# Attention feeding a capacity-limited expert layer: a coarse-grid routing search with an exact count, and row turning moved to VectorE

## The chip, the cores and the metric

The kernel runs on one core of one Trainium2 chip. A core has a matrix engine (TensorE, "PE" in the profile; its weight loads are "PEld"), three elementwise engines (VectorE "DVE", ScalarE "ACT", GpSimd "POOL"), a queue engine that issues transfers (SyncE, "SP" or "SPq"), an on-chip memory of 128 partitions, a matmul result memory (PSUM) and 16 DMA engines that reach DRAM. Every engine works through its own list of instructions in order; semaphores order them against each other. The metric is device time in microseconds of one execution.

## The reference

```python
def _attn_ref(q, k, v):                     # 8 batches, 12 heads, 448 tokens, 64
    scores = scale * np.matmul(q, k.transpose(0, 1, 3, 2)) - np.log(S)
    attn = 1.0 / (1.0 + np.exp(-scores))
    return np.matmul(attn, v)

def _moe_ref(x, w_gate, w1, w2):            # x: 3584 tokens x 768; 8 experts, 768 -> 1024 -> 768
    cap = N // E                            # 448
    logits = x @ w_gate
    order = np.argsort(-logits.flatten())
    for idx in order:                       # best (token, expert) pair first
        tok, e = idx // E, idx % E
        if assigned[tok] >= 0 or counts[e] >= cap: continue
        assigned[tok] = e; counts[e] += 1
    for e in range(E):
        mask = assigned == e
        out[mask] = np.maximum(x[mask] @ w1[e], 0.0) @ w2[e]
```

The attention uses a sigmoid in place of a softmax. Its output, one row of 768 numbers per token, goes to the expert layer. Each of the 3584 tokens goes to one of 8 experts, and each expert takes exactly 448, in the order of all logits. All values are 32-bit floats.

## The kernel before, in words

**Attention.** 48 pairs of heads (8 batches of 6) run one after the other. For a pair, VectorE turns k and q (`kqT`, L408), ScalarE and VectorE split them into a high and a low part (`kqH` L416, `kqL` L417), TensorE forms the scores (L433, L443), ScalarE the sigmoid (L423), TensorE the product with v (L457, L463), and VectorE copies the result to `xt` (L465, L467). `xt` holds a batch with its 768 features on partitions. A short list `bg` holds work that is slipped in, one item for each pair: the logits of a finished batch (L478, L480), and for batch 0 the function `rows`: three transposes on TensorE (L489), a copy, and after two of them a store of 112 token rows to the DRAM tile `xs` (L496). For the other seven batches (`LATE = 7`) these 56 items wait in the list `late`.

**Routing** goes in eight phases; a phase finds the expert that fills first among those left. `keys` gives a token's logit to its best expert and a very low number to the others, and two transposes put the keys of the experts on partitions (`r_KE`, 16 partitions for each expert). `search` finds, for all experts at once, the bit pattern of the 448th largest key, two bits a step, in 16 steps: three counts of keys at or above a threshold (L178, each followed by a read of its accumulator), a sum over the expert's 16 partitions (in phase 0 a small matmul, L190; later two VectorE transposes and a reduce, L194 to L200), and the next thresholds (L202 to L217). `pick` takes the expert with the highest threshold (L229 to L250), `place` and `lists` (L257 to L298) make the list of its 448 tokens.

**Phase 0 stands alone** between attention and experts. In its loop (L563) some of the `late` items are put on TensorE and ScalarE after every step: one before, seven after the keys, three after each search step. When the expert is known, SP reads its number (`value_load`, L585) and issues the loads of its weights (L592); when the list is known, GpSimd gathers the token rows (L625), and `xturn` transposes them back on TensorE (L639) and splits them (L642 on ScalarE, L643 on VectorE).

**Experts.** Eight times, 144 matmuls for the first layer (L734, L736, L738) and 144 for the second (L771, L773, L775). The order of everything else is fixed when the program is written out, by a clock that adds 189 for each matmul: at `t_route` the next piece of the routing of a later phase is put in, then the clock must advance by the number the piece returned (`T_STEP`, `T_DVE`, `T_PICK` and so on) plus `SLACK`; `chores` hold the gathers and `xturn`s of the next expert and the transposes of finished outputs (L652), with a due time each, one in 1000. `prepare` enters the gathers and turns of the next expert as soon as its list is known; what is left at the end of an expert is put out by `flush`.

Of the kernel before, what the change touches and what calls it, by code (L numbers as in the profile page):

```python
# [7 lines left out]
F32 = mybir.dt.float32  # L8
F32R = mybir.dt.float32r
BF = mybir.dt.bfloat16  # L10
# [12 lines left out]
LATE = 7  # L23
XT_BUFS = 7
# [5 lines left out]
T_KEYS, T_KE, T_STEP, T_DVE, T_KAP, T_PICK, T_TOT, T_OH, T_BT = 3600, 2100, 2050, 2025, 500, 2600, 600, 3800, 600  # L30
# [6 lines left out]
Y_DVE, Y_WAIT = 6, 4000  # L37

# [10 lines left out]
def route_consts(nc, cp, K):  # L49
# [59 lines left out]
    g = 0  # L109
# [6 lines left out]
    K.gfin = _s32(g)  # L116


class Router:
# [4 lines left out]
    def __init__(self, tc, K, st, wk, psum):  # L124
# [5 lines left out]
        tc.nc.vector.memset(self.csum, -28.0)  # L130

# [30 lines left out]
    def search(self, pe):  # L162

        nc, K, wk, KT = self.nc, self.K, self.wk, self.KT
        p = self.bank()
        for g in range(2):
            nc.tensor.transpose(p[:, g * 112:(g + 1) * 112],
                                KT[:, g].rearrange("p e c -> p (e c)"), K.ident[:112, :112])
        KE = wk.tile([128, 224], F32, name="r_KE")
        nc.vector.tensor_copy(KE, p[:, :224])  # L170
        T, JP = K.c0, None
        X = None if pe else self.bank().bitcast(I32)
        for st in range(16):
            sh = 30 - 2 * st
            cnt = wk.tile([128, 3], BF, name="r_cnt") if pe else K.CN
            for i in range(3):
                junk = wk.tile([128, 224], BF, name="r_junk")
                nc.vector.tensor_scalar(junk, KE, T[:, i:i + 1].bitcast(F32), None, OP.is_ge, OP.add,  # L178
                                        accum_out=cnt[:, i:i + 1])
            nX = None  # L180
            if 0 < st < 15:
                nX = wk.tile([128, 3], I32, name="r_X") if pe else X[:, 4 * (st % 2):4 * (st % 2) + 3]
            acc = wk.tile([128, 1], F32, name="r_acc")
            j2 = wk.tile([128, 3], F32, name="r_j2")
            if pe:
                if nX is not None:
                    nc.vector.tensor_scalar(nX, K.kk[:, st + 1], JP, None, OP.bitwise_xor)
# [4 lines left out]
            else:  # L192
                ct = wk.tile([128, 32], F32, name="r_ct")
                nc.vector.transpose(ct, cnt)  # L194
                if nX is not None:
                    nc.vector.tensor_scalar(nX, K.kk[:, st + 1], JP, None, OP.bitwise_xor)
                s2 = wk.tile([128, 2], F32, name="r_s2")
                nc.vector.tensor_reduce(s2, ct.rearrange("p (e r) -> p e r", r=16), AX.X, OP.add)
                ct2 = wk.tile([128, 32], F32, name="r_ct")
# [19 lines left out]
            if not pe:  # L219
                yield T_DVE  # L220
# [666 lines left out]
```

## Time and profile before

| | |
|---|---|
| median of 3 runs | 882.02 us (881.35 to 885.34) |
| the profiled execution | 883.43 us, span 881.7 us, mean granted clock 0.987 |
| attention | from 0 to 278.6 us |
| phase 0 of the routing, first loads, gather and turns | 278.6 to 332.8 us |
| experts | 332.8 to 861 us |
| the last rows out | 861 to 881.7 us |
| busy: PE, DVE, ACT, POOL | 840.1, 542.4, 447.3, 466.0 us |
| bytes read, written in DRAM | 96.76 MB, 24.31 MB |

The stages are read off the instructions in order of time: the last logits of attention stand at 278.7 us, the first expert matmul at 332.8 us. A busy TensorE need not be at its full rate, since its matmuls overlap and their ends are modelled. In the rows "x18" counts instructions that were merged, the bracket behind a row gives the idle time of its engine before it and what ended it, and a row of a stretch gives, for each engine, microseconds busy and the number of instructions, then the granted TensorE clock (1.00 is full), the share of the DMA engines that was busy, and GB/s.

### The profile page before, as it was taken

What the parts mean: (1) busy time and instruction counts of PE and PEld (TensorE: products, weight loads), DVE (VectorE), ACT (ScalarE), POOL (GpSimd) and SP (SyncE); (2) the same over time, 40 slices, a digit from 0 to 9 for tenths busy, and PEclk for the clock granted to TensorE, in tenths of its full rate; (3) what the DMA queues carried; (4) which work ended last, traced back from release to release, by engine and by line L of the source; (5) the groups of instructions that cost most, each with busy time, mean ns of one, the idle gap of its engine ahead of it and who ended that gap; (6) DMA issues with size and microseconds to landing.
All of it is one profiled execution on the core that took longest, in us unless ns stands there. A gap on an engine that the chain in (4) does not pass through costs nothing.

```text
span 881.7 us, 16211 instructions
## 1 busy us (share of the span) xinstructions
PE 840.1 (95%) x5467; PEld 636.9 (72%) x5467; DVE 542.4 (62%) x2060; ACT 447.3 (51%) x612; POOL 466.0 (53%) x446
## 2 busy tenths in 40 slices
PE   6999999999999739998999999999999999999996
PEld 3455555555554528987988988988888888999996
DVE  4566555555554988958859879779779631332130
ACT  6777677777775734434434434534434344541420
POOL 9744344444410014854864873873883883851561
PEclk9999999999999979998999999999999999999999
DMA  9866766666621855443442442551542542634643
GB/s 173 165 142 149 153 126 127 127 126 127 126 43 54 270 192 154 120 138 123 128 136 97 160 155 81 177 162 57 189 153 72 170 153 90 209 96 141 203 151 126
DMA packets 213811, 122.16 MB, mean 139 GB/s; under 512 B 153344, under 2 KB 202496, under 8 KB 213728
## 3 DMA queue, kind: packets, MB, share of 16 engines
q1 hardware_dynamic: 200992, 87.62, 38.2%
q0 software_dynamic: 10880, 33.28, 12.0%
q8 instruction: 43, 0.70, 0.3%
q10 hardware_dynamic: 1856, 0.23, 0.2%
q14 instruction: 40, 0.33, 0.1%
HBM read 96.76 MB, written 24.31 MB: 137 GB/s over the span
## 4 chain that ended last, share of the span: by engine, by line
PE 82%; DVE 11%; issue 2%; DMA 2%; POOL 1%; SPq 1%; ACT 1%; POOLq 0%; DVEq 0%; ACTq 0%
PE tp L457 13%; PE sc L433 11%; PE sc L736 9%; PE sc L734 9%; PE sc L738 9%; PE sc L773 6%; PE sc L775 6%; PE sc L771 6%; DVE r_junk L178 4%; PE tp L463 2%; PE sc L443 2%; PE tp L639 2%; PE tp L652 2%; PE tp L478 1%; PE rt L289 1%
## 5 line engine op out<-in xcount | busy, mean ns | idle before, releaser
L605 POOL TENSOR_TENSOR wl<-wr,wh 128x768 fp32r<-128x768 f32 (+1 forms) x96 | 204.9, 2145 | 124.5 <-ACT wh L603 116.8
L423 ACT ACTIVATE at<-sc,bias 128x896 f32<-128x896 f32 x168 | 161.5, 1006 | 67.1 <-PE sc L443 38.4
L383 POOL DMA_DIRECT2D nkq<-in_q_dram x188 | 118.4, 646 | 116.2 <-DVE kqT L408 104.6
L775 PE MATMUL sc<-hh,wl 128*128 128x448 f32 (+2 forms) x400 | 150.2, 375 | 0.0
L738 PE MATMUL sc<-xh,wl 128*128 128x448 f32 (+2 forms) x396 | 146.2, 369 | 0.0
L736 PE MATMUL sc<-xl,wh 128*128 128x448 f32 (+2 forms) x396 | 146.0, 369 | 0.1
L773 PE MATMUL sc<-hl,wh 128*128 128x448 f32 (+2 forms) x400 | 145.5, 364 | 0.2 <-POOL hl L746 0.2
L734 PE MATMUL sc<-xh,wh 128*128 128x448 f32 (+2 forms) x396 | 145.0, 366 | 0.0
L771 PE MATMUL sc<-hh,wh 128*128 128x448 f32 (+2 forms) x400 | 144.1, 360 | 0.4 <-issue 0.4
L178 DVE TENSOR_SCALAR_CACHE_REDUCE r_junk<-r_KE,r_T 128x224 bf16<-128x224 f32 x315 | 123.2, 441 | 0.1
L603 ACT ACTIVATE wh<-wr 128x768 fp32r<-128x768 f32 (+1 forms) x112 | 102.0, 939 | 36.3 <-DMA wr<-in_moe_w_dram 23.4
L457 PE MATMUL tp<-at,nv 128*64 128x448 f32 x576 | 118.8, 548 | 0.0
L746 POOL TENSOR_TENSOR hl<-yt,hh 128x896 fp32r<-128x896 f32 x32 | 68.4, 2136 | 48.8 <-ACT yt L745 47.2
L742 ACT ACTIVATE hh<-sc 128x896 fp32r<-128x896 f32 x32 | 29.5, 921 | 117.1 <-PE sc L738 117.1
L417 DVE TENSOR_TENSOR kqL<-kqT,kqH 128x896 fp32r<-128x896 f32 (+1 forms) x49 | 52.5, 1073 | 58.5 <-ACT kqH L416 58.4
L773 PEld LDWEIGHTS sc<-hl,wh 128*128 128x128 f32 x400 | 75.8, 189 | 6.8 <-issue 1.1
L625 POOL DMA_INDIRECT xr<-xs,r_idx x32 | 32.0, 999 | 91.2 <-ACT wh L603 80.2
L736 PEld LDWEIGHTS sc<-xl,wh 128*128 128x128 f32 x396 | 75.2, 190 | 6.7 <-issue 0.5
L457 PEld LDWEIGHTS tp<-at,nv 128*64 128x64 f32 x576 | 37.1, 136 | 59.1 <-issue 56.6
L734 PEld LDWEIGHTS sc<-xh,wh 128*128 128x128 f32 x396 | 75.2, 190 | 6.0
L771 PEld LDWEIGHTS sc<-hh,wh 128*128 128x128 f32 x400 | 76.0, 190 | 4.8 <-issue 0.6
L738 PEld LDWEIGHTS sc<-xh,wl 128*128 128x128 f32 x396 | 75.1, 190 | 5.3
(166 smaller groups left out, 1266.1 us busy)
## 6 DMA issues: line engine op xcount, KB each, us to landing
wr<-in_moe_w_dram SPq DMA_DIRECT2D x64, 384.0 KB, 3.0
wr<-in_moe_w_dram SPq DMA_DIRECT2D x48, 512.0 KB, 3.6
nkq<-in_k_dram SPq DMA_DIRECT2D x192, 56.0 KB, 2.6
xs<-xr SPq DMA_DIRECT2D x32, 336.0 KB, 3.3
nkq<-in_q_dram POOLq DMA_DIRECT2D x188, 56.0 KB, 2.7
nv<-in_v_dram SPq DMA_DIRECT2D x92, 96.0 KB, 2.7
ys<-yt SPq DMA_DIRECT2D x20, 112.0 KB, 1.9
nr<-in_v_dram SPq DMA_DIRECT2D x46, 32.0 KB, 2.2
```

Source lines behind the costliest of these rows:

```text
L178: nc.vector.tensor_scalar(junk, KE, T[:, i:i + 1].bitcast(F32), None, OP.is_ge, OP.add, accum_out=cnt[:, i:i + 1])
L383: qn.dma_start(t[o:o + 32, n], rws[x])
L423: nc.scalar.activation(a, p[:, :, :S], AF.Sigmoid, bias=bias, scale=1 / math.sqrt(D))
L457: nc.tensor.matmul(p[j * 64:j * 64 + 64, :S], nat["v", b, g][:, h0 + j, c, :], AT[b, pr, c][:, j, :], start=(c == 0), stop=(c == 2 and pr ...
L603: nc.scalar.activation(hi, raw[u], AF.Copy)
L605: eng.tensor_tensor(lo, raw[u], hi.bitcast(F32), OP.subtract)
L734: nc.tensor.matmul(ph[:, f, lo:hi], wh[:, a, fs], xh[:, dd, lo:hi], start=st, stop=False)
L736: nc.tensor.matmul(ph[:, f, lo:hi], wh[:, a, fs], xl[:, dd, lo:hi], start=False, stop=False)
L738: nc.tensor.matmul(ph[:, f, lo:hi], wl[:, a, fs], xh[:, dd, lo:hi], start=False, stop=en)
L771: nc.tensor.matmul(py[:, d2, :w], wh[:, a, dsl], h1, start=st, stop=False)
L773: nc.tensor.matmul(py[:, d2, :w], wh[:, a, dsl], h2, start=False, stop=False)
L775: nc.tensor.matmul(py[:, d2, :w], wl[:, a, dsl], h1, start=False, stop=(j == 1 and a == 3))
```

## The change

**Search.** Thresholds are now numbers on a grid, not bit patterns. `scale`, which runs once in the attention, takes `D`, the power of two at or below the largest logit of batches 0 to 3. Phase 0 starts at -2D with steps of D and refines four times by 4 (`N_FIRST`), so it ends on a multiple of D/64. Each later phase starts at the last phase's threshold less D and takes nine steps (`N_FAST`), down to D/262144. Each step has three counts, the sum, and three small operations, as before. Then one more count at the point found (`count(base)`) gives the exact number of keys at or above it.

**Pick.** Thresholds and counts are spread over the partitions by a transpose and a matmul; `pick` leaves out experts with fewer than 448, takes the highest, and adds the counts of those that have this threshold. If the sum is exactly 448, the tokens above the threshold are the expert's tokens. VectorE reads this sum into a register (`value_load`) and branches: if it is not 448, `exact` does the former 16-step search in one piece on VectorE.

**Rows.** Batches 0 to 6 are no longer transposed by TensorE. After every second pair `turn_rows` does one VectorE transpose of 32x32 blocks (128x2x448, 896 numbers on each partition), three for a batch; it writes every sixth number of the tile `xz` (24 bytes apart), and after the third SP stores the batch with four transfers. A token's row in `xs` now has its 768 features in another order (feature r*128+c at 6c+r), so that `xturn` reads its operand with a step of six numbers, and the `late` rows of batch 7, the only ones left (`LATE = 1`), are copied into this order too.

**Order.** `T_PICK` is 7000 in place of 2600, `T_KAP` 1500 in place of 500, and `prepare` enters gathers and turns no earlier than 33000 into an expert (`X_AT`), the first expert excepted. Tiles: `xt` 3 buffers in place of 7, `xz` 2.

```diff
-LATE = 7
-XT_BUFS = 7
+LATE = 1
+XT_BUFS = 3
+XZ_BUFS = 2
-T_KEYS, ..., T_KAP, T_PICK, ... = 3600, 2100, 2050, 2025, 500, 2600, 600, 3800, 600
+T_KEYS, ..., T_KAP, T_PICK, ... = 3600, 2100, 2050, 2025, 1500, 7000, 600, 3800, 600
+N_FIRST, N_FAST = 4, 9
+FOUND = 0x43E00000
+X_AT = 33000
...
-        for st in range(16):
+    def search(self, k):
+        pe = k == 0
+        rows = range(N_FIRST) if pe else range(1, N_FAST + 1)
...
+        for r in rows:
+            cnt = wk.tile([128, 3], BF, name="r_cnt") if pe else K.CN
+            for i in range(3):
+                self.count(T[:, i:i + 1], cnt[:, i:i + 1])
...
+            nc.vector.tensor_scalar(j2, tot, 447.5, None, OP.is_ge, OP.add, accum_out=acc)
+            if more:
+                T = wk.tile([128, 3], F32, name="r_T")
+                nc.vector.scalar_tensor_tensor(T, acc.to_broadcast([128, 3]), K.kw[:, r, :1], nX, OP.mult, OP.add)
+            nb = wk.tile([128, 1], F32, name="r_base")
+            nc.vector.tensor_scalar(nb, acc, K.kw[:, r, :1], base, OP.mult, OP.add)
+            base = nb
+            if more and not pe:
+                yield T_DVE
+        self.base = base
+        self.cnt = wk.tile([128, 1], BF, name="r_cn1")
+        self.count(base, self.cnt)
...
     def pick(self):
-        nc.tensor.transpose(p[:112, :128], self.kap.to_broadcast([128, 112]), K.ident)
+        nc.tensor.transpose(p[:, :128], self.base.to_broadcast([128, 128]), K.ident)
+        nc.tensor.matmul(p[:, 128:256], self.cnt.to_broadcast([128, 128]), K.G, start=True, stop=True)
+        nc.vector.tensor_scalar(few, cr, 447.5, NONE, OP.is_lt, OP.mult)
+        nc.vector.tensor_tensor(kr, tr, few, OP.subtract)
         nc.vector.tensor_reduce(km, kr, AX.X, OP.max)
+        nc.vector.tensor_tensor(few, cr, few, OP.add)
+        nc.vector.scalar_tensor_tensor(few, kr, km, few, OP.is_equal, OP.mult)
+        nc.vector.tensor_reduce(ok, few, AX.X, OP.add)
+        found = nc.vector.value_load(ok[:1].bitcast(I32))
+        with self.tc.If(found != FOUND):
+            self.exact(kr)
+            nc.vector.tensor_reduce(km, kr, AX.X, OP.max)
...
+        def turn_rows(b, pr):
+            if pr == 1:
+                XR[b] = xa.tile([128, S // 32, 32, NP], F32, name="xz", bufs=XZ_BUFS)
+            nc.vector.transpose(XR[b].rearrange("p i j r -> p r i j")[:, pr - 1:pr + 1],
+                                XT[b][:, pr - 1:pr + 1].rearrange("p r (i t) -> p r i t", t=32))
+            if pr == NP - 1:
+                for a in range(4):
+                    nc.sync.dma_start(xs[b * S:(b + 1) * S, 192 * a:192 * a + 192].rearrange("(i t) c -> t i c", t=32),
+                                      XR[b][32 * a:32 * a + 32].rearrange("t i j r -> t i (j r)"))
...
+            if old and old[1] % 2 and old[0] < B - LATE:
+                bg.append(lambda b=old[0], pr=old[1]: turn_rows(b, pr))
...
-                nc.tensor.transpose(p[:, i * n:(i + 1) * n], xg[kx, j][:n, dd * 128:(dd + 1) * 128], ident[:n, :n])
+                nc.tensor.transpose(p[:, i * n:(i + 1) * n], xg[kx, j][:n, dd::NP], ident[:n, :n])
...
             def prepare():
-                t0 = clock[0]
+                t0 = max(clock[0], start + X_AT) if kx else clock[0]
```

**VectorE at the end of phase 0**, before: the last of 16 search steps and the pick (`r_junk` is a count, `r_km` the highest threshold).

```order
L178 TENSOR_SCALAR r_junk,r_cnt<-r_KE,r_T 128x224 x3
L202 TENSOR_SCALAR r_j_3968,r_acc<-rt 128x3
L217 TENSOR_SCALAR r_J<-r_acc,r_J 128x1
L222 TENSOR_SCALAR r_kap<-r_J 128x1
L232 TENSOR_REDUCE r_km<-rt 112x1
L234 SCALAR_TENSOR_TENSOR r_w_3998<-rt,r_km,c_rank 112x8
```

And now: the last of 4 steps and the pick, to the branch over `exact`.

```order
L183 TENSOR_SCALAR r_junk,r_cnt<-r_KE,r_T 128x224 x3
L233 TENSOR_SCALAR r_j_3514,r_acc<-rt 128x3
L238 TENSOR_SCALAR r_base<-r_acc,c_kw,c_base_2069 128x1
L183 TENSOR_SCALAR r_junk,r_cn_3520<-r_KE,r_base 128x224
L290 TENSOR_SCALAR r_few<-rt 128x8
L291 TENSOR_TENSOR r_kr<-rt,r_few 128x8
L293 TENSOR_REDUCE r_km<-r_kr 128x1
L294 TENSOR_TENSOR r_few<-rt,r_few 128x8
L295 SCALAR_TENSOR_TENSOR r_few<-r_kr,r_km,r_few 128x8
L297 TENSOR_REDUCE r_ok<-r_few 128x1
L298 TENSOR_LOAD r_ok
L299 COMPARE_AND_BRANCH
```

Twelve steps are gone; one count, five small operations, a register load and a branch stand before the row that was L234 and is L304 now.

**TensorE at the end of expert 0**, before: the last second-layer matmuls of expert 0, the turns of expert 1's rows (`xr`), and the first-layer matmuls of expert 1.

```order
L639 MATMUL tp<-ident,xr 128x128 x3
L775 MATMUL sc<-hh,wl 128x448
L771 MATMUL sc<-hh,wh 128x448
L773 MATMUL sc<-hl,wh 128x448
L775 MATMUL sc<-hh,wl 128x448
L639 MATMUL tp<-ident,xr 128x128 x9
L639 MATMUL tp<-ident,xr 128x64 x6
L734 MATMUL sc<-xh,wh 128x448
```

And now, where the last two of the eight turns stand.

```order
L872 MATMUL sc<-hl,wh 128x448
L738 MATMUL tp<-ident,xr 128x64 x3
L874 MATMUL sc<-hh,wl 128x448
L870 MATMUL sc<-hh,wh 128x448
L872 MATMUL sc<-hl,wh 128x448
L874 MATMUL sc<-hh,wl 128x448
L870 MATMUL sc<-hh,wh 128x448
L872 MATMUL sc<-hl,wh 128x448
L738 MATMUL tp<-ident,xr 128x64 x3
L874 MATMUL sc<-hh,wl 128x448
```

Five of the eight turns stood behind the last matmul of expert 0; now all eight stand among its matmuls, six apart, the last well before its end.

**VectorE in the attention**, now: the work of two pairs, with the turn of `xt` between the copy of one pair and the turn of k and q for another.

```order
L536 COPY xt<-tp 128x448
L589 STREAM_TRANSPOSE xz<-xt 128x2x448
L479 STREAM_TRANSPOSE kqT<-nkq 128x896
L488 TENSOR_TENSOR kqL<-kqT,kqH 128x896
L536 COPY xt<-tp 128x448
L538 TENSOR_TENSOR xt<-tp,xt 128x448
```

Before, the same rows stood there without `xz`, and in batch 1's time a copy of `rows` after some of them. The logits of a finished batch, which were the first item slipped in behind it, are now the second, one pair later.

More of the change, by code (lines that the diff above doesn't have):

```diff
@@ L116, in route_consts @@
     K.gfin = _s32(g)
+    K.cw = cp.tile([128, N_FAST + 1, 3], F32, name="c_cw")
+    for r in range(N_FAST + 1):
+        nc.vector.tensor_scalar(K.cw[:, r], t8, 4.0 ** -r, None, OP.mult)
 class Router:
@@ L160, in keys, with ends @@
         self.KT = KT
-    def search(self, pe):
-        nc, K, wk, KT = self.nc, self.K, self.wk, self.KT
+    def ends(self):
+        nc, KT = self.nc, self.KT
         p = self.bank()
@@ L167, in search @@
             nc.tensor.transpose(p[:, g * 112:(g + 1) * 112],
[L168 to L172, printed above, removed]
-        for st in range(16):
-            sh = 30 - 2 * st
+                                KT[:, g].rearrange("p e c -> p (e c)"), self.K.ident[:112, :112])
+        self.KE = self.wk.tile([128, 224], F32, name="r_KE")
@@ new lines, in ends, with count, sums @@
+        nc.vector.tensor_copy(self.KE, p[:, :224])
+    def count(self, T, cnt):
+        junk = self.wk.tile([128, 224], BF, name="r_junk")
+        self.nc.vector.tensor_scalar(junk, self.KE, T, None, OP.is_ge, OP.add, accum_out=cnt)
+    def sums(self, cnt, ct, s2, ct2, between=None):
+        nc = self.nc
+        nc.vector.transpose(ct, cnt)
+        if between:
+            between()
+        nc.vector.tensor_reduce(s2, ct.rearrange("p (e r) -> p e r", r=16), AX.X, OP.add)
+        nc.vector.transpose(ct2.rearrange("p (e r) -> p e r", r=16), s2[:, :, None].to_broadcast([128, 2, 16]))
+        return ct2[:, :3]
@@ L185, in search @@
             if pe:
[L186 to L187 removed]
+                ahead()
                 yield T_STEP
@@ L192, in search @@
             else:
[L193 to L199, printed above, removed]
-                nc.vector.transpose(ct2.rearrange("p (e r) -> p e r", r=16), s2[:, :, None].to_broadcast([128, 2, 16]))
@@ L225, in pick @@
+        nc.vector.tensor_copy(f[0], nX[:, :1].bitcast(F32).to_broadcast([128, 32]))
+        nc.vector.transpose(f[1], f[0])
+        for q in range(4):
+            for o in range(4):
+                nc.vector.tensor_copy(kr[32 * o:32 * o + 32, 2 * q:2 * q + 2], f[1][32 * q:32 * q + 32, ::16])
     def pick(self):
@@ L329, in phase @@
             yield T_KEYS
-            yield from self.search(k == 0)
+            self.ends()
+            yield from self.search(k)
             yield T_KAP
```

106 lines of the change are left out of this document (70 added, 36 removed).

## The prediction

> **What bounds the kernel now.** I read the chain of waits first, then the stretches of the stages, then each stage's instructions in time. The first row below is the chain's share by engine, then come the stretches of the first three stages (PE, PEld, DVE, ACT and POOL busy, clock, DMA share, GB/s), with two short ones that are used later.
>
> ```profile
> PE 82%; DVE 11%; issue 2%; DMA 2%; POOL 1%; SPq 1%; ACT 1%; POOLq 0%; DVEq 0%; ACTq 0%
> ```
>
> ```profile
> 0.00:278.60 278.60, 270.40 (x2216) 137.88 (x2216) 152.91 (x210) 200.34 (x220) 128.30 (x220) 1.00 0.62 125
> 278.60:332.80 54.20, 34.27 (x257) 22.89 (x257) 44.72 (x222) 29.14 (x61) 4.13 (x6) 0.87 0.69 220
> 332.80:861.00 528.20, 522.35 (x2891) 463.76 (x2890) 342.69 (x1625) 215.65 (x325) 329.48 (x213) 0.99 0.44 137
> 320.00:325.00 5.00, 1.32 (x34) 1.05 (x34) 3.23 (x8) 1.63 (x2) 0.00 (x0) 0.50 0.46 157
> 405.00:410.00 5.00, 4.68 (x15) 4.07 (x16) 4.09 (x23) 1.42 (x3) 1.86 (x2) 0.50 0.01 2
> ```
>
> TensorE sets the pace of attention (270.4 of 278.6 us busy, the rest is the start) and of the experts (522.4 of 528.2). Only in the 54 us between them does it wait, and there VectorE is busy 44.7. This stretch is phase 0, one dependent chain. Its rows in time: the first count, the second step, the last step, its end, the threshold, the highest threshold, and the operation behind it.
>
> ```profile
> 285.12 0.45 DVE L178 TENSOR_SCALAR_CACHE_REDUCE r_junk<-r_KE,c_c 128x224 bf16<-128x224 f32 x1
> ...
> 287.66 0.45 DVE L178 TENSOR_SCALAR_CACHE_REDUCE r_junk<-r_KE,r_T 128x224 bf16<-128x224 f32 x1
> ...
> 313.51 0.44 DVE L178 TENSOR_SCALAR_CACHE_REDUCE r_junk<-r_KE,r_T 128x224 bf16<-128x224 f32 x1
> ...
> 315.16 0.21 DVE L217 TENSOR_SCALAR r_J<-r_acc,r_J 128x1 int32<-128x1 int32 x1
> 315.40 0.15 DVE L222 TENSOR_SCALAR r_kap<-r_J 128x1 int32<-128x1 int32 x1
> ...
> 315.97 0.17 DVE L232 TENSOR_REDUCE r_km<-rt 112x1 f32<-112x8 f32 x1 [0.41 <-PE rt L229]
> 316.17 0.23 DVE L234 SCALAR_TENSOR_TENSOR r_w<-rt,r_km,c_rank 112x8 f32<-112x8 f32 x1
> ```
>
> From 287.66 to 313.51 are 14 steps, 1.846 us each, and L234 starts 31.05 us after the first count. What follows is a chain too, by the chain's own rows: nothing of the weights or rows is asked for before the pick, so it moves with it.
>
> ```profile
> 320.44 3.76 DMA wr<-in_moe_w_dram
> ...
> 326.70 4.49 DMA xr<-xs,r_idx
> ```
>
> **The change, part by part.**
>
> *Search and pick of phase 0.* The new steps have the same counts, the same matmul and as many small operations, so three cost 1.846 each, 5.54 (the old first step, 2.54, had three operations that are gone). The fourth runs to its last operation as the old last step did (313.51 to 315.16, plus 0.2: 1.85). Then one count more with its read (0.55); the hop to TensorE and back (from 315.40, where the old threshold was formed, to 315.97: 0.55); six small operations at the 0.20 between 315.97 and 316.17, with some of them longer (1.3); a register load and a branch. SP loads a register from the same kind of tile, in the row of the load and the register operation behind it (shortest/median/longest in ns, then first and last start):
>
> ```profile
> L585 SPq TENSOR_LOAD <-r_ei x8: 266/278/481, 318.4 to 796.1; - x8
> L585 SPq FUSED_REGOPS  x8: 152/157/181, 319.0 to 796.4; - x8
> ```
>
> From 318.4 to 319.0 is 0.6 us, and 0.15 for the compare; with the jumps 0.9. No row shows a jump. Below I bound it by nothing, above by the 1.9 us that the shortest of the profile's transfers takes to land, as if code had to be fetched:
>
> ```profile
> ys<-yt SPq DMA_DIRECT2D x20, 112.0 KB, 1.9
> ```
>
> I take 0.15, the register operation's row, as both are sequencer work. [...]
>
> Sum: 5.54 + 1.85 + 0.55 + 0.55 + 1.3 + 0.9 = 10.7 in place of 31.05, a gain of 20.35. TensorE has no late rows left to do in these steps, so it falls to the clock of the 320 to 325 row (0.50), and its five small matmuls on the chain, 0.16 to 0.32 us each, grow by about 0.3 in all. **Gain 20.0**, with bounds 18 and 20.5.
>
> *Rows of batch 0 off TensorE.* Eight groups of three transposes stood in the attention; the first and the last:
>
> ```profile
> 56.40 0.54 PE L489 MATMUL tp<-ident,xt 128*112 128x128 f32 x3
> ...
> 95.92 0.54 PE L489 MATMUL tp<-ident,xt 128*112 128x128 f32 x3
> ```
>
> 8 × 0.54 = 4.3, on the pace-setter. `scale` gives some back once: TensorE waits for the 0.62 copy (below), two small VectorE operations, and does one transpose, with hops 1.7. **Gain 2.6.** The 48 other groups ran under the search and pay nothing by going.
>
> *Rows by VectorE.* 21 transposes of 896 numbers. Each goes between a copy (L465) and the next kqT; around that place:
>
> ```profile
> 240.65 0.62 DVE L465 COPY xt<-tp 128x448 f32<-128x448 f32 x1 [0.53 <-PE tp L457]
> ...
> 241.19 1.10 DVE L408 STREAM_TRANSPOSE kqT<-nkq 128x896 f32<-128x896 f32 x1
> ...
> 243.37 1.09 DVE L417 TENSOR_TENSOR kqL<-kqT,kqH 128x896 fp32r<-128x896 f32 x1 [1.08 <-ACT kqH L416]
> ...
> 246.62 0.47 PE L433 MATMUL sc<-kqH 64*128 64x448 f32 x2
> 246.84 1.01 ACT L423 ACTIVATE at<-sc,bias 128x896 f32<-128x896 f32 x1 [1.71 <-PE sc L443]
> ```
>
> The same transpose with contiguous writes takes 1.10, and with writes 8 bytes apart, on the outputs of the last experts, 1.12:
>
> ```profile
> L669 DVE STREAM_TRANSPOSE yt<-sc x5: 1117/1119/1119, 792.9 to 861.7; 128x896 f32<-128x896 f32 x5
> ```
>
> The lower bound is 1.10, the upper, for 24 bytes apart, twice that. kqL, 1.10 later, ends at 245.6, and the scores that need it start at 246.62. ScalarE waits 1.1 for kqH and then has 1.71 idle. So kqL comes 1.0 us before TensorE asks for it, and kqT could be 2.1 late in all. I put it at **nothing**, by the L669 row; at 2.2 each it would cost 0.1 × 21 = 2.
>
> *Stores.* SP now has 28 issues in the attention, before 4. Eight loads of k, in as many pieces each as a store has, take it 4.18 us, 0.52 each; and from 40 to 250 us it waits (us in total, times, longest) on kqT alone 26 us:
>
> ```profile
> 74.61 4.18 SPq L383 DMA_DIRECT2D nkq<-in_k_dram  x8
> ```
>
> ```profile
> SPq L383 <- DVE kqT L408: 26.2, 13, 3.2
> ```
>
> 28 × 0.52 = 15 fits into 26. Behind a store on SP's queue stand the loads of k and v for pairs three to four ahead, some 17 us before their use (278.6 / 48 = 5.8 for a pair). **Nothing**, with the DMA engines themselves left to a rival.
>
> *End of expert 0.* Expert 1's list came late, so five of its eight turns stood in a row after expert 0:
>
> ```profile
> 400.44 0.36 PE L775 MATMUL sc<-hh,wl 128*128 128x448 f32 x1
> 401.88 1.01 PE L639 MATMUL tp<-ident,xr 128*128 128x128 f32 x6 [1.08 <-DVE xl L643]
> ...
> 405.83 0.74 PE L734 MATMUL sc<-xh,wh 128*128 128x448 f32 x1
> ```
>
> From 400.64, where the next matmul was due, to 405.83 are 5.2 us; spread out, five turns cost 0.33 each (below), 1.7, so 3.5 are lost. Then the clock is at half: 15 matmul records in the row from 405 to 410, where 5 us hold 24, 2.0 more. With 9 steps in place of 16 the list of expert 1 is out 8,000 to 10,000 of the clock's units sooner, and the order has the turns among the matmuls. **Gain 5.5**, bounds 3 and 6.
>
> *Later phases.* The six later searches lose 42 steps, but VectorE (342.7 of 528.2 busy) is not the bound there: nothing. Their branches hold VectorE 0.9 us each, twice just ahead of turns: **loss 0.5**, bounds 0 and 12 (six times the 2 us).
>
> *Turns with a step of six numbers.* 64 groups of three transposes now load weights 24 bytes apart. What a group costs now is read between matmuls:
>
> ```profile
> 725.36 0.37 PE L773 MATMUL sc<-hl,wh 128*128 128x448 f32 x1
> 725.56 0.49 PE L639 MATMUL tp<-ident,xr 128*128 128x128 f32 x3
> ...
> 726.09 0.36 PE L771 MATMUL sc<-hh,wh 128*128 128x448 f32 x1
> ```
>
> 725.36 to 726.09 less two matmuls at 0.20 is 0.33. The nearest rows with a step are the weight loads of the second layer, contiguous in expert 3 (560 to 592 us, first row) and 8 bytes apart in expert 6 (800 to 812, second); mean ns behind the comma:
>
> ```profile
> L771 PEld LDWEIGHTS sc<-hh,wh 128*128 128x128 f32 x22 | 4.1, 188 | 0.3
> ```
>
> ```profile
> L771 PEld LDWEIGHTS sc<-hh,wh 128*128 128x128 f32 x19 | 3.7, 194 | 0.2
> ```
>
> 3% more. Bounds: nothing, and a doubling, 64 × 0.33 = 21. I take **nothing**, the end that these rows are nearest to. [...]
>
> **Sum.** 883.4 - 20.0 - 2.6 - 5.5 + 0.5 = 855.8 for an execution like the profiled one. That one stood 1.4 above the median, so 854.4; I say **855**. The bounds that do not belong to a rival make it 850 to 862.
>
> **The rivals.**
>
> *The branch is taken.* I worked the reference's logits out in double precision from its inputs. D is 2^-6 (largest logit 0.01696). Phase 0 finds its grid point easily, and five later phases have a gap of 2.7e-7 or more, or none behind the 448th key, against a grid of 6.0e-8. In phase 4 the gap between keys 448 and 449 is 4.0e-8; a grid point lies in it, 1.2e-8 above the lower key. Logits larger by two parts in a million miss it. Then `exact` holds VectorE for 16 steps of the pitch in these chain rows, 2.33 us, and 20 small copies, 41 us:
>
> ```profile
> 657.17 1.11 DVE r_junk L178 x6
> 659.50 1.11 DVE r_junk L178 x6
> ```
>
> The order puts this pick 0.41 of an expert into expert 2, its turns for expert 3 at 0.75; an expert takes 68 us, so the turns wait until 1.01, some 17 us of TensorE, and then come in a burst that costs some 3 as at 400 us. 855 + 20 = **875**. For it: the narrow margin. Against: the sigmoid's error must be one-sided and of that size.
>
> *The step of 24 bytes costs* (the slower rival). Place: the weight loads of the turns, in line with TensorE's matmuls, and VectorE's new transposes. Price, where each takes f times as long: 21 × (f - 1) us for the turns, and 21 times what 1.1 × f exceeds 2.1 by. 1.5 gives 866, 2 gives **878**, and from 2.2 (25 + 6) the kernel is slower than before, 886. For it: no row has a step as long. Against: 188 and 194, 1.10 and 1.12. [...]
>
> *The DMA engines.* The stores of batches 0 to 6 come in 12,544 pieces of 768 bytes. Two rows show what a packet takes, of loads in the attention (100 to 250 us) and of the old stores (282 to 315): packets, MB, share of 16 engines.
>
> ```profile
> q1 hardware_dynamic: 77625, 12.76, 45.7%
> ```
>
> ```profile
> q1 hardware_dynamic: 3294, 8.88, 83.2%
> ```
>
> 14 ns for 164 bytes, 133 for 2,700. By bytes a piece of 768 takes 38 ns, in all 30 us of 16 engines, 0.11 of the stage; at 133 ns it would be 104 us, 0.37, which with the 0.62 there now makes 1.0. Then loads come 1 to 2 us late for each of six batches: **865**. For it: k's loads stand behind the stores on one queue. Against: shorter pieces take less time.
>
> **How the numbers follow.** The forecast 0.61; branch taken 0.18; the step 0.14 (0.03 of it slower, 0.04 no change); DMA engines 0.05; others 0.02. The range reaches from 848, where the rest of the experts' 5.8 us without TensorE goes too (some 3 us), to **877**, to take in the taken branch; the forecast's own is 850 to 862. A difference under 0.5% (877.6 to 886.4 is no change) can't be told from none: faster 0.91, same 0.05, slower 0.04.
>
> **What would show it.** Four steps of 1.85 us between attention and the experts, and 10 to 11 us from the first count to L304; attention 2 to 3 us shorter with TensorE never waiting on kqL; no burst of L738 near 400 us and no clock of 0.5 after it; a group of L738 at 0.49; no `x_f` tile at work anywhere. A run of L183 counts without pauses in expert 2, an L738 group at 0.7 or more, or a `xz` transpose above 2.1 us would make the forecast wrong.

## The result: slower, 896.0 us where 855 was predicted

The changed kernel takes 896.0 us (median of 4 runs, 891.0 to 897.4) beside 882.3 for the kernel before: 1.0144 times as long, interval 1.0102 to 1.0186. The profiled execution took 897.4 us with a span of 895.6, against 881.7. Four rows of TensorE in time cut both spans into the same stages: the last logits of attention and the last block of second-layer matmuls, before and after (the experts' first matmul stands at 332.80 before and at 324.69 now).

```profile
278.71 0.59 PE L478 MATMUL tp<-xt,wgz 128*32 128x112 f32 x16 [0.82 <-DVE xt L467]
872.24 0.36 PE L771 MATMUL sc<-hh,wh 128*128 128x192 f32 x1 [0.41 <-issue]
```

```profile
286.97 0.59 PE L549 MATMUL tp<-xt,wgz 128*32 128x112 f32 x16 [0.82 <-DVE xt L538]
324.69 0.56 PE L833 MATMUL sc<-xh,wh 128*128 128x256 f32 x1
886.14 0.36 PE L870 MATMUL sc<-hh,wh 128*128 128x192 f32 x1 [0.41 <-ACT yt L802]
```

| stage (us) | before | after | difference | predicted | missed |
|---|---|---|---|---|---|
| attention, to the last logits | 278.7 | 287.0 | +8.3 | -2.6 | 10.9 |
| to the experts' first matmul | 54.1 | 37.7 | -16.4 | -20.0 | 3.6 |
| to the last block of the experts | 539.4 | 561.5 | +22.0 | -5.0 | 27.0 |
| rest | 9.5 | 9.5 | 0 | 0 | 0 |

So the search did become shorter, and more than that was lost before and behind it.

**Attention loses its time in the first 40 us**, before `xz` is first stored. Stretches of the kernel before, then of the changed one (columns as in the prediction: PE, PEld, DVE, ACT, POOL busy, clock, DMA share, GB/s):

```profile
0.00:20.00 20.00, 12.51 (x78) 7.35 (x80) 8.29 (x10) 12.68 (x16) 19.16 (x37) 1.00 0.91 170
30.00:40.00 10.00, 10.00 (x74) 4.94 (x72) 5.63 (x10) 7.64 (x9) 6.27 (x11) 1.00 0.91 181
```

```profile
0.00:20.00 20.00, 10.31 (x58) 5.38 (x58) 6.74 (x9) 10.22 (x13) 17.77 (x35) 1.00 1.17 144
30.00:40.00 10.00, 6.51 (x34) 2.90 (x30) 6.50 (x6) 6.02 (x7) 6.17 (x17) 0.83 0.80 137
100.00:250.00 150.00, 148.07 (x1217) 75.16 (x1215) 104.48 (x119) 112.39 (x122) 67.68 (x108) 1.00 0.94 164
```

TensorE has done 20 matmuls fewer by 20 us, and 40 fewer between 30 and 40, where its clock drops. The DMA engines are busier and move less: 144 GB/s at a share of 1.17, against 170 at 0.91. The rows of that start: the changed kernel's two waits for operands of the scores, then the load queue's own row over the first 45 us (packets, MB, share), of the changed kernel and of the one before.

```profile
33.36 0.47 PE L504 MATMUL sc<-kqH 64*128 64x448 f32 x2 [2.84 <-ACT kqH L487]
34.49 0.47 PE L504 MATMUL sc<-kqL,kqH 64*128 64x448 f32 x2 [0.65 <-DVE kqL L488]
```

```profile
q1 hardware_dynamic: 25310, 3.52, 73.7%
```

```profile
q1 hardware_dynamic: 29936, 4.32, 57.0%
```

16 engines for 45 us, times the share, by the packets: 21 ns a packet of 139 bytes now, 13.7 for 144 bytes before. The loads are the same; their destinations are not. The change's new small tiles (constants, and those of `exact`) stand ahead of the tiles of q, k and v and move these by 1,600 bytes: `nkq` began at byte 57,600 of a partition, a multiple of 256, and begins at 59,200, 64 bytes past one.

**The routing before the experts.** VectorE's rows: the first count, the sum of the proof, and the operation behind the branch; then the sequencer's load, compare and the semaphore behind the jump (shortest/median/longest in ns, first and last start).

```profile
294.31 0.45 DVE L183 TENSOR_SCALAR_CACHE_REDUCE r_junk<-r_KE,c_T 128x224 bf16<-128x224 f32 x1
...
303.96 0.16 DVE L297 TENSOR_REDUCE r_ok<-r_few 128x1 f32<-128x8 f32 x1
307.88 0.23 DVE L304 SCALAR_TENSOR_TENSOR r_w<-r_kr,r_km,c_rank 112x8 f32<-112x8 f32 x1 [3.76 <-DVEq L299]
```

```profile
L298 DVEq TENSOR_LOAD <-r_ok x7: 315/320/547, 304.2 to 603.0; - x7
L299 DVEq COMPARE_BRANCH  x7: 63/63/72, 304.8 to 603.4; - x7
L299 DVEq EVENT_SEMAPHORE  x7: 21/21/21, 307.8 to 607.3; - x7
```

From first count to L304 are 13.57 us, not 10.7. The load and the compare are as cheap as forecast; between the compare (304.8) and what follows (307.8) 3.0 us pass without an instruction. `exact` did no work in any phase.

**The experts.** What TensorE waited for among them (us in total, times, longest), before and after:

```profile
PE tp L639 <- DVE xl L643: 4.2, 5, 1.1
PE rt L167 <- DVE r_KT L158: 0.6, 2, 0.3
```

```profile
PE tp L738 <- DVE xl L742: 8.5, 4, 3.9
PE rt L286 <- DVE r_base L238: 4.7, 4, 1.4
PE rt L327 <- DVE r_ei L319: 2.8, 2, 2.0
PE rt L176 <- DVE r_KT L167: 1.2, 4, 0.3
```

The burst of turns behind expert 0 is gone, as predicted, but the waits are longer than before. The costliest, row by row: VectorE's branch, the remainder `xl` queued behind it, TensorE's wait for that, and the clock after it.

```profile
607.46 0.23 DVE L304 SCALAR_TENSOR_TENSOR r_w<-r_kr,r_km,c_rank 112x8 f32<-112x8 f32 x1 [4.53 <-DVEq L299]
...
609.77 1.00 DVE L742 TENSOR_TENSOR xl<-tp,xh 128x384 fp32r<-128x384 f32 x2
```

```profile
610.36 0.93 PE L738 MATMUL tp<-ident,xr 128*128 128x128 f32 x3 [3.90 <-DVE xl L742]
```

```profile
610.00:615.00 5.00, 4.64 (x15) 4.19 (x16) 1.59 (x4) 0.98 (x2) 0.00 (x0) 0.50 0.00 0
```

Theory after this reading: four causes add up to the 41 us missed. The addresses slow the first loads; each jump over `exact` holds VectorE for 3 us or more; the step of 24 bytes makes the turns dearer; and the pieces of the routing stand too early on TensorE's list. The rivals are given with each run.

### The profile page after: what moved, and what is told of

It reads as the page before. It is cut to its first block, busy times and chain, and to the rows that moved or that the text cites. A ratio compares the mean times of both kernels' runs of the same rounds, so it can differ in the third digit from the quotient of the medians.

```text
span 895.6 us, 15137 instructions
## 1 busy us (share of the span) xinstructions
PE 827.4 (92%) x5295; PEld 631.3 (70%) x5295; DVE 481.1 (54%) x1417; ACT 429.5 (48%) x564; POOL 465.9 (52%) x446
## 5 line engine op out<-in xcount | busy, mean ns | idle before, releaser
L872 PE MATMUL sc<-hl,wh 128*128 128x448 f32 (+2 forms) x400 | 151.7, 379 | 0.0
L874 PE MATMUL sc<-hh,wl 128*128 128x448 f32 (+2 forms) x400 | 147.6, 369 | 0.0
L742 DVE TENSOR_TENSOR xl<-tp,xh 128x384 fp32r<-128x384 f32 (+1 forms) x60 | 29.4, 503 | 126.4 <-ACT xh L741 126.1
L874 PEld LDWEIGHTS sc<-hh,wl 128*128 128x128 f32 x400 | 77.3, 193 | 4.7 <-issue 0.4
```

Of the source, the lines that this page charges most:

```text
L872: nc.tensor.matmul(py[:, d2, :w], wh[:, a, dsl], h2, start=False, stop=False)
L874: nc.tensor.matmul(py[:, d2, :w], wl[:, a, dsl], h1, start=False, stop=(j == 1 and a == 3))
```

## The experiments

### Addresses

The changed kernel, its tiles moved back to multiples of 256 bytes:

```diff
         bias = cp.tile([128, 1], F32, name="bias")
+        padding = cp.tile([128, 48], F32, name="padding")
+        nc.gpsimd.memset(padding[:1, :1], 0.0)
```

> The changed kernel with an unused tile of 192 bytes a partition after the constants, so that all tiles behind it start at multiples of 256 bytes, as they do before the change; nothing else differs. Theory (a change of the tiles' addresses by 1,600 bytes slowed the loads into them): the loads of q and k land in about 2.6 us instead of 3.6 and 4.0, the attention's last logits end at 276 to 279 instead of 287, and the whole takes 884 to 888 us. Rival (the stores in 768-byte pieces and the turns of 1.85 us slow the attention): the landings stay at 3.6 and 4.0, the last logits at 287, the time at 894 to 898.

Measured 886.5 us (884.8 to 887.6), 9.5 less, last logits at 278.90; q's loads take 2.9 us to land, not 4.0 (medians over the whole profile). Of the profiled executions the attention is 8.1 shorter and the experts are 3.5 shorter (558.0 us). The same edit in the kernel before, with `[128, 16]` and with `[128, 32]`:

> The kernel before with an unused tile of 64 bytes after the constants, so that its tiles start 64 bytes off a multiple of 256, as they do after the change; nothing else differs. Theory (addresses): the loads of q and k land in about 3.6 to 4.0 us instead of 2.6 and 2.7, the last logits end at 287 to 290 instead of 278.7, and the time is 890 to 895 us. Rival (stores and turns): 2.6 and 2.7, 278.7, and 881 to 884 us.

> The kernel before with an unused tile of 128 bytes after the constants: its tiles start 128 bytes off a multiple of 256. Theory (what costs is that a piece of 256 bytes does not start at a multiple of 256): as with 64 bytes, loads of q and k landing in 3.1 to 3.7 us, last logits at 285 to 288, 889 to 893 us. Rival (only starts that are no multiple of 128 cost): 2.6 and 2.7, 278.7, 881 to 884 us.

64 bytes: 891.0 us, 1.0088 times the kernel before (1.0057 to 1.0119), last logits at 286.02, loads of k and q landing in 3.1 and 3.7 us, a little less than forecast. 128 bytes: 884.2 us, 1.0013 (1.0000 to 1.0026), last logits at 279.46, landings of 2.6 and 2.7. The start in the changed kernel moved back, and in the one before moved by 64:

```profile
0.00:20.00 20.00, 12.61 (x78) 7.32 (x80) 8.21 (x10) 12.62 (x16) 19.17 (x38) 1.00 0.91 172
30.00:40.00 10.00, 10.00 (x74) 4.90 (x74) 6.94 (x12) 7.96 (x9) 6.35 (x11) 1.00 0.90 182
100.00:250.00 150.00, 148.04 (x1221) 74.85 (x1215) 104.94 (x120) 113.07 (x123) 66.97 (x107) 1.00 0.77 164
```

```profile
0.00:20.00 20.00, 10.83 (x60) 5.83 (x62) 7.04 (x9) 10.56 (x13) 17.84 (x36) 1.00 1.17 143
30.00:40.00 10.00, 7.04 (x40) 3.46 (x42) 4.91 (x5) 6.44 (x7) 7.41 (x19) 0.83 1.09 157
```

The address does it in both kernels and both ways; stores and slow turns (the rival) are in the first and not in the second. Two starts off a multiple of 256 were tried, no others: 64 bytes past one cost 8 us and more, 128 bytes past one 1.3. My theory had the limit at 256, the rival at 128, and the rival holds in the main, though 884.2 is 0.2 above its range. No run shows why such a start costs time. The load queue's share in the first 45 us was 57.0% in the kernel before, 62.3% at 128 bytes and 76.9% at 64. Later the pace is the same (1,217 and 1,221 matmuls from 100 to 250 us), though the DMA engines are busy 0.94 instead of 0.77: there the loads are ahead of their use, and the cost in the attention is the start and the gap of 2.84 us, with a clock of 0.83 from 30 to 40 us where the aligned kernel has 1.00.

### The branch

Without value load, branch and `exact` (addresses kept):

```diff
-        found = nc.vector.value_load(ok[:1].bitcast(I32))
-        with self.tc.If(found != FOUND):
-            self.exact(kr)
-            nc.vector.tensor_reduce(km, kr, AX.X, OP.max)
```

> The changed kernel without the value load, the branch and the 16-step search behind it (the proof is still computed, nobody reads it; an unused tile of 448 bytes keeps all addresses as they were). Theory (each branch keeps VectorE from its next instruction for about 3 us, and among the experts TensorE comes to wait for VectorE): the routing before the first expert becomes 3.5 to 4.5 us shorter, TensorE's gaps among the experts fall from 17 us to under 8, and the time is 878 to 885 us. Rival (the branch costs only where TensorE waits for the routing, before the first expert): the experts take the 550 us they take now, and the time is 891 to 893 us.

879.4 us (877.2 to 880.4), 16.6 less. The experts take 548.0 us instead of 561.5; TensorE is idle for 10.0 of them instead of 18.4, more than the 8 forecast. From the first count of phase 0 to the operation on the winner there are 9.7:

```profile
293.92 0.45 DVE L183 TENSOR_SCALAR_CACHE_REDUCE r_junk<-r_KE,c_T 128x224 bf16<-128x224 f32 x1
...
303.64 0.22 DVE L300 SCALAR_TENSOR_TENSOR r_w<-r_kr,r_km,c_rank 112x8 f32<-112x8 f32 x1
```

Then only the body was cut to its last line (addresses kept):

```diff
         with self.tc.If(found != FOUND):
-            self.exact(kr)
             nc.vector.tensor_reduce(km, kr, AX.X, OP.max)
```

> The changed kernel with the 16-step search left out of the branch's body, which keeps one instruction, so that the jump over it is short; the value load, the compare and the branch stay, and an unused tile of 448 bytes keeps all addresses (without the search the guard no longer finds the exact value where the grid misses it, which does not happen with these inputs). Theory one (the 3 us are what a jump over the long body costs): VectorE is idle for under 1 us ahead of the winner row instead of 3.76, and the time is 879 to 883 us, as without the branch. Theory two (any branch costs this, however far it jumps): the idle time stays at 3.5 to 4.0 us and the time at 894 to 897.

882.2 us (880.6 to 886.4). So the load, the compare and the branch cost 2.8 of the 16.6 by the medians, and what the branch jumps over costs the rest. Last, `exact` was written shorter with the guard whole, in the aligned kernel: up to 15 thresholds in one operation, 91 rows of VectorE's program in place of 180 (the part that matters):

```diff
...
-        for st in range(16):
-            sh = 30 - 2 * st
-            for i in range(3):
-                self.count(T[:, i:i + 1].bitcast(F32), K.CN[:, i:i + 1])
+        for st, sh in enumerate((30, 28, 24, 20, 16, 12, 8, 4, 0)):
+            n = 3 if sh > 24 else 15
+            nc.vector.tensor_tensor(big[:, :n], self.KE[:, None, :].to_broadcast([128, n, 224]),
+                                    T[:, :n].bitcast(F32)[:, :, None].to_broadcast([128, n, 224]), OP.is_ge)
+            nc.vector.tensor_reduce(K.CN[:, :n], big[:, :n], AX.X, OP.add)
...
```

> The changed kernel with all tiles back on multiples of 256 bytes and the guard whole, its exact search written in 9 steps of up to 15 thresholds, so that the branch jumps over 91 of VectorE's rows instead of 180. Theory one (a jump over half the length finds its target already loaded, as the jump over one row does): VectorE is idle for 1.0 to 1.5 us ahead of the winner row, and the time is 872 to 875 us. Theory two (the cost grows with the length): 2 to 2.5 us, 876 to 880. Theory three (whatever leaves the first few rows costs it all): 3.8 us, 884 to 888.

877.1 us (875.1 to 877.4). VectorE's wait behind the branch over the seven phases (total, times, longest), for 180 rows, 1 row and 91 rows; with the last two, the compare and the semaphore behind the jump:

```profile
DVE r_w L304 <- DVEq L299: 27.6, 7, 4.5
```

```profile
DVE r_w L303 <- DVEq L299: 5.5, 7, 1.0
L299 DVEq COMPARE_BRANCH  x7: 56/56/72, 302.2 to 589.3; - x7
L299 DVEq EVENT_SEMAPHORE  x7: 21/21/21, 302.5 to 589.6; - x7
```

```profile
DVE r_w L294 <- DVEq L289: 7.4, 7, 1.4
L289 DVEq COMPARE_BRANCH  x7: 56/63/72, 295.8 to 585.4; - x7
L289 DVEq EVENT_SEMAPHORE  x7: 21/21/21, 296.4 to 586.0; - x7
```

3.9, 0.8 and 1.1 us each: 91 rows are nearly as cheap as one (theory one's idle time; what is loaded no row shows), 180 are not. The time came out 2 above theory one, within theory two's range, because the small rest still makes `xl` late once (2.1 us at the end of expert 3, with a clock of 0.66 in the 5 us behind it). What the guard costs where it is needed was measured by taking the branch always:

```diff
-        with self.tc.If(found != FOUND):
+        with self.tc.If(found != 0):
```

> As the aligned kernel with the guard over 91 rows, but the branch into the exact search is always taken, in all seven phases: what the guard costs where it is needed. Estimate from the rows of the page (0.44 us for a count of 224 numbers, so about 6.6 us for fifteen, and a sum of the same size behind it): 9 to 13 us a full step, 60 to 90 us a phase. In phase 0 all of it lies on the path; among the experts VectorE's own work of 30 to 50 us a phase comes on top of it, so that the experts wait: 1,200 to 1,450 us in all.

1,388 us in a single run, as estimated: 511 more, 73 a phase.

### The step of 24 bytes

In `xz`, in `turn_rows` and in the turn's operand, so that both engines use consecutive numbers (two of the edits):

```diff
-                XR[b] = xa.tile([128, S // 32, 32, NP], F32, name="xz", bufs=XZ_BUFS)
+                XR[b] = xa.tile([128, S // 32, NP, 32], F32, name="xz", bufs=XZ_BUFS)
...
-                nc.tensor.transpose(p[:, i * n:(i + 1) * n], xg[kx, j][:n, dd::NP], ident[:n, :n])
+                nc.tensor.transpose(p[:, i * n:(i + 1) * n], xg[kx, j][:n, dd * 128:(dd + 1) * 128], ident[:n, :n])
```

> The changed kernel with the six numbers of a feature group laid so that both VectorE's turn writes and TensorE's turn of the rows reads consecutive numbers; stores, counts of instructions and addresses stay. The features reach the experts in another order than their weights, so the output differs; the work is the same. Theory (the step of 24 bytes costs the turns of the rows 0.055 us per full group and 0.22 us per half group, and VectorE's slower turns lie in its idle time): a turn in the attention takes 1.1 us instead of 1.85, the last logits end at 287 as before, the experts get 5 to 7 us shorter, and the time is 888 to 891 us. Rival one (the step costs TensorE nothing that is waited for): 895 to 897 us. Rival two (the slow turns of 1.85 us hold up the attention): its last logits end at 279 to 283.

887.7 us (881.8 to 891.2), 8.3 less. Weight loads of the turns among the experts and VectorE's turn in the attention (mean ns behind the comma), with the step and without:

```profile
L738 PEld LDWEIGHTS tp<-ident,xr 128*128 128x128 f32 x126 | 23.1, 222 | 11.4 <-DVE xl L742 10.5
L589 DVE STREAM_TRANSPOSE xz<-xt 128x896 f32<-128x896 f32 x21 | 38.8, 1850 | 0.0
```

```profile
L737 PEld LDWEIGHTS tp<-ident,xr 128*128 128x128 f32 x126 | 16.5, 146 | 13.7 <-DVE xl L741 10.1 <-DMA xr<-xs,r_idx 0.6
L588 DVE STREAM_TRANSPOSE xz<-xt 128x896 f32<-128x896 f32 x21 | 23.1, 1102 | 0.0
```

From the matmul ahead of a group of three turns to the one behind it are 0.51 us with the step and 0.45 without; for the groups of 64 tokens 0.85 and 0.62. 48 × 0.06 + 16 × 0.23 = 6.6 us in all; 44 and 16 of these groups stand among the experts, 6.3 us, and the experts took 4.6 less (561.5 to 556.9). The profile of this run also had no drop of the clock in the first 40 us (1.00 from 30 to 40; last logits at 281.7), although its loads were as slow (144 GB/s at a DMA share of 1.18 in the first 20 us, beside 144 at 1.17); the gap was 1.77 us there, so the attention part of the 8.3 was not settled here. The next two kernels, both aligned by 128 bytes of padding and without the branch, the second with consecutive numbers too, settle it:

> Both at once: no value load, branch and 16-step search, and an unused tile of 128 bytes, which puts all tiles back on multiples of 256 bytes. Theory (the two losses lie in different stages, 9.5 us in the first 40 us of the attention and 16.6 us in the routing and among the experts, and add up): 868 to 872 us, attention's last logits at 278 to 280, experts as without the branch. Rival (a kernel that waits less at one place waits at the next): 873 to 878.

> As the aligned kernel without the branch, with the six numbers of a feature group laid so that the turns write and read consecutive numbers (the features then meet the weights in another order, so the output differs, the work not). Theory (the step of 24 bytes costs the experts 4.5 to 6 us on TensorE and nothing elsewhere): 5 to 6 us below the aligned kernel without the branch, 863 to 867 us. Rival (most of the 8 us that consecutive numbers gave came from the start of the attention, which the addresses have mended already): within 2.5 us of it, 868 to 871.

871.4 us (871.1 to 873.4) and 864.0 (862.2 to 864.7). Addresses and branch add up nearly: 886.5 - 15.1, where the branch alone gave 16.6. The last logits of the two:

```profile
278.82 0.59 PE L547 MATMUL tp<-xt,wgz 128*32 128x112 f32 x16 [0.82 <-DVE xt L536]
```

```profile
276.46 0.59 PE L547 MATMUL tp<-xt,wgz 128*32 128x112 f32 x16 [0.82 <-DVE xt L536]
```

The step is worth 7.4, more than the theory had, and not only where it had it: VectorE's 0.75 us more for each turn cost 2.4 in the attention of these two. Over all profiled kernels that are aligned the last logits stand at 278.0 to 278.9 with the step and at 276.4 to 276.8 without. The routing takes 33.4 and 32.5, the experts 547.7 and 544.4.

### What is left among the experts

With 864 against 855 the experts still took 544.4 us, where 534.4 had been predicted. In four phases TensorE waited 1.0 to 1.4 us for the base of the search. The planner's number between last step and pick was moved from 1,500 to 3,500 and to 2,500 (`T_KAP`), in the aligned kernel with the guard over 91 rows:

```diff
-T_KEYS, T_KE, T_STEP, T_DVE, T_KAP, ... = 3600, 2100, 2050, 2025, 1500, ...
+T_KEYS, T_KE, T_STEP, T_DVE, T_KAP, ... = 3600, 2100, 2050, 2025, 2500, ...
```

> As the aligned kernel with the guard over 91 rows, with the planner's time between the last search step and the pick at 3,500 instead of 1,500 ns, so that TensorE's two instructions of the pick stand about 2 us of matmuls later in the experts. Theory (TensorE came to these two before VectorE had the last base: four or five waits of 1.0 to 1.4 us, and the clock behind them): the waits on the base fall under 0.3 us each and the time is 5 to 8 us below the kernel with 1,500. Rival (the waits go to the next instruction that TensorE shares with VectorE's routing): within 2 us of it.

> As the aligned kernel with the guard over 91 rows, with 2,500 ns between last search step and pick in place of 1,500, which is about what the list before had between them. Theory (TensorE's waits on the base of 1.06, 1.37, 1.25 and 1.37 us are lost time, and 3,500 was only too much): these waits fall under 0.4 us, those on xl stay at 4 us, and the time is 871 to 874. Rival (a moved pick pushes VectorE's other work later, whatever the amount): 876 to 880, with more waits on xl.

879.8 us (876.7 to 883.1), 2.7 more, and 871.0 (870.7 to 871.1), 6.1 less than the 877.1 with 1,500. TensorE's waits among the experts for 1,500, 3,500 and 2,500:

```profile
PE rt L276 <- DVE r_base L231: 5.0, 4, 1.4
PE tp L730 <- DVE xl L734: 4.1, 3, 2.1
```

```profile
PE tp L730 <- DVE xl L734: 10.1, 6, 2.7
PE rt L349 <- DVE r_oh L344: 2.1, 2, 1.1
PE rt L317 <- DVE r_ei L309: 1.5, 1, 1.5
```

```profile
PE tp L730 <- DVE xl L734: 5.3, 5, 1.9
PE rt L276 <- DVE r_base L231: 0.2, 1, 0.2
```

1 us later takes the waits on the base away; 2 us later moves them to the remainders, which queue behind the pick on VectorE. Both the theory and the rival hold, each at its distance. Consecutive numbers on top of 3,500:

> As the run with the pick two us later, and the turns write and read consecutive numbers (the features then meet the weights in another order, so the output differs, the work not). Theory (address, jump, step and the pick's place are the whole of what the prediction missed): 854 to 859 us, about the predicted 855. Rival (something else is left among the experts): 861 or more.

875.3 us (873.4 to 876.5), 4.5 less and far from 855: the rival, something else was left. Next the change's due time for the turns, set to 0 and to 27,000:

```diff
-X_AT = 33000
+X_AT = 0
```

> As the aligned kernel with the guard over 91 rows, with the change's edit of the due times undone: the turns of the next expert's rows are due as soon as its routing is out, as before the change, not from 33,000 of the planner's nanoseconds on. Theory (held back, the turns wait for VectorE's remainders at the end of each expert: 4.1 us of waits on xl and the clock at half behind one of 2.1 us): the waits on xl shrink to under 2 us and the time falls by 3 to 6 us, to 871 to 874. Rival (the turns meet VectorE's search or DMA gathers elsewhere): within 2 us of 877 or above it.

> As the aligned kernel with the guard over 91 rows, with the turns of the next rows due from 27,000 of the planner's nanoseconds into an expert, not 33,000. Theory (the later the turns, the more they wait for VectorE's remainders): between the kernel with no holding back and the one with 33,000. Rival (the due time does not matter where the routing is out later than that anyway): 876 to 878, as with 33,000.

875.9 (875.5 to 876.8) and 880.9 us (879.4 to 882.2) beside 877.1. Holding the turns back is not what costs; my theory of it falls. The 880.9 lies outside what theory and rival gave for 27,000, and why a due time between the two is the worst stays open. Last the sum, with the pick 1 us later and consecutive numbers, with and without the guard:

> As the run with the pick 1 us later (aligned, guard over 91 rows), and the turns write and read consecutive numbers (the features then meet the weights in another order, so the output differs, the work not). Theory (the step of 24 bytes costs 4.5 to 7 us wherever the rest stands): 864 to 867 us. Rival (with TensorE's waits on the base gone, the shorter turns of the rows only bring it to VectorE's remainders earlier): 868 to 871.

> Aligned, without value load, branch and exact search, the pick 1 us later, and consecutive numbers in the turns: every cost of the change that the runs have named is taken out. Theory (they add up to what the prediction missed): 4 to 6 us below the aligned kernel without a branch and with consecutive numbers, 858 to 860 us, near the predicted 855. Rival (without the branch VectorE reaches the base early enough, and the later pick only delays it): 863 to 866.

866.4 us (863.3 to 868.0) and 858.3 (857.8 to 859.7). With the guard, consecutive numbers give 4.6 by the medians, as the theory says, but in the profiled executions the experts take 546.2 and 545.8: there the rival is right, the shorter turns only meet VectorE's remainders earlier. Without the guard the theory holds. This last kernel has no guard and its features meet the weights in another order: it shows where the time went and is not one to use. From the changed kernel to the last, in the order in which they were taken out: addresses 9.5, branch 15.1, step 7.4, place of the pick 5.8, in all 37.7 of the 41 us. In another order the shares shift: without the branch the addresses are worth 8.0. The aligned kernel with the whole guard over 91 rows and the pick 1 us later, at 871.0, is faster than both kernels: 0.9867 times the one before (0.9845 to 0.9888).

## Why the prediction was wrong

**Right.** *Search and pick of phase 0*: without load and branch the first count stands at 293.92 and the operation on the winner at 303.64, 9.7 us, where the sum without these two was 9.8 (10.7 less 0.9); with addresses and step mended too the stage took 32.5 us instead of 54.1. *Rows of batch 0*: with addresses and step mended the last logits stand at 276.5, 2.3 earlier, against 2.6. That leaves at most 0.3 for the *stores*, put at nothing; the DMA engines' share from 100 to 250 us rose from 0.63 to 0.77 in the aligned kernel, 0.14, near the 0.11 that the rival had by bytes, and its 10 us later loads did not come. *The branch is not taken*, as the forecast had it.

**A term that the sum did not have: the addresses, 9.5 us.** No step asked what the new tiles ahead of the load buffers do to the places where transfers land. I read the change for what it computes, and a tile that nobody in the attention uses was costed at nothing without a thought.

**"No row shows a jump ... I take 0.15": it was 3.0 to 3.9 us** from the compare to the next event in the first and last phase; on average VectorE idled 3.2 us longer than behind the one-row jump ((27.6 - 5.5) / 7). The upper bound of 1.9, the shortest transfer's landing, was too low for one jump, and I chose the wrong end: a sequencer operation that stays in line is no neighbour of one that jumps over 180 rows. The runs show a wait of VectorE of 3.4 to 4.5 us at each of the seven jumps over 180 rows, and 0.3 us more over 91 rows than over one (1.1 and 0.8 on average). What passes in it no row shows; that code is fetched there, which my upper bound assumed, is not shown either. In phase 0 this is 3 of the 3.6 us that the second line of the table missed.

**"Their branches hold VectorE 0.9 us each ... loss 0.5, bounds 0 and 12": 13.5 us among the experts.** The mechanism was named, and its size followed from the price of the jump: six jumps held VectorE 23.8 us (27.6 less 3.8), and more than half of it reached the end: 8.4 us as idle time of TensorE, the rest as slower work. `xl` waits behind the branch, TensorE behind `xl`, and behind the gap of 3.9 us stand 5 us at half clock (0.50). In the row of 610 to 615 us are 15 matmuls, where 5 us at full clock hold 24 (one in 0.20 to 0.21 us in its rows at 500 and 725 us).

**"Turns with a step of six numbers: nothing": 4.5 to 8.3 us by the medians of four pairs of runs.** My nearest rows had a step of 8 bytes. The slower rival named the place, and its factors of 1.5 to 2.2 were assumed, not read from a row; here the weight load grew from 146 to 222 ns and the transpose from 1.10 to 1.85 us, but the sum came nowhere near its upper end of 21. A full group cost 0.06 more on 0.33, a group of 64 tokens 0.23 more on 0.42 (0.62 less a matmul), so f was 1.2 and 1.5, not 2. The transpose stayed under its bound of 2.2 us, and yet 2.4 us went in the attention: the cover of 2.1 that I read at one place is not there in every pair. Two waits of TensorE of 0.5 us, on `kqL` and on a copy into `xt`, stand in the profile with the step and not in the one without; what makes up the other 1.4 stays open.

**"End of expert 0: gain 5.5".** The burst went, as the row by row reading had it, but little time with it. In the last run, with every named cost taken out, the experts take 537.9 us: 1.5 less than before, not 5.0. Waits for `xl` elsewhere (4.0 us, 4.2 before) took its place, and TensorE is idle for 6.8 us, 6.3 before.

```profile
308.65:846.59 537.94, 531.15 (x2988) 472.51 (x2986) 267.55 (x1081) 217.06 (x328) 332.50 (x217) 1.00 0.44 138
```

I priced the end of one wait and not what a list with other places brings.

**"The six later searches ... nothing": 5.8 us.** VectorE was not the bound by its share, but the pick's two TensorE instructions moved ahead of the base they need. 5.8 is what 1 us more gave in the last pair of kernels, 6.1 in the one with the guard. Before, a step's `T_DVE` and 500 stood between last step and pick; now 1,500 do. The order showed that and I did not price it.

The chances were wrong in the same way: faster at 0.91 rested on terms that were read well, while the rivals held only causes with a row in the profile before.

## What to carry to other kernels

Ask of a change also what it moves without meaning to: addresses of the tiles behind a new one, and the place of instructions on a list that is fixed when the program is written. A branch that was never taken cost here by what it jumps over, 0.8, 1.1 and 3.9 us of VectorE's wait for 1, 91 and 180 rows: keep the rare path short, or test at a place where nobody waits for that engine. Price a stall by what queues behind it on its engine and by the clock after it (0.50 for 5 us behind the one of 3.90), not by its own length.

## What the hardware did that I had not expected

With the tiles 64 bytes past a multiple of 256 a packet of some 140 bytes took 21 ns, with the tiles on one 13.7, and 128 bytes past one 14.8. A jump over one row left 0.3 us between compare and the next event, over 91 rows 0.6, over 180 rows 3.0 in the first phase and 3.9 in the last; no lengths between were tried. At the start of the attention TensorE's clock fell behind gaps of 2.30, 2.69 and 2.84 us (0.83 from 30 to 40 us behind the first and the last; behind the other a row of two matmuls took 0.57 us instead of 0.37) and stayed at 1.00 behind 1.77 and 2.25, each with a second gap of 0.65 us about 1 us later. With the same addresses the last logits stand at 284.4 us behind the gap of 2.25 and at 286.6 behind that of 2.69, so 0.44 us more of a gap went with 2.2 us more in the attention. What decides between the two stays open. The 3.3 us between 858.3 and the forecast lie among the experts, where the last run took 3.5 more than predicted; what they are stays open too.
